# The opening of a Fourier-then-experts kernel on one core: units copied by two engines, a new order of its tail, and two transfer queues reordered

## The chip, the core and the metric

The kernel runs on one core of a Trainium2 chip. The core has a matrix engine (TensorE, PE in the profile, with its weight loads as PEld), a vector engine (VectorE, DVE), a scalar engine (ScalarE, ACT), a general engine (GpSimd, POOL) and a queue engine (SyncE, SP) that here only issues transfers. Each engine works through its own list of instructions in order. The engines share two memories on the core: SBUF, and PSUM, into which alone the matrix engine writes and which has eight banks of 128 x 512 floats. Sixteen DMA engines move data between these and DRAM. Transfers issued by SP stand in the profile as queue q1 (hardware_dynamic), those issued by POOL as queue q0 (software_dynamic).

The metric is the device time of one execution in microseconds. Before the change the median of three runs is 879.62 us (879.46 to 879.99).

## The reference

`x` has 8 batches of 3008 rows by 256. Each batch goes through a real FFT over the rows, a complex 256 x 256 product with bias, a soft threshold at 0.01, and the inverse FFT. The result, 24064 x 256, goes through two dense layers (256 to 2048 to 256) with an ELU between them.

```python
X = np.fft.rfft(x, axis=1)
Yr = Xr @ w_r - Xi @ w_i + b_r
Yi = Xr @ w_i + Xi @ w_r + b_i
Yr = np.sign(Yr) * np.maximum(np.abs(Yr) - lam, 0.0)
Yi = np.sign(Yi) * np.maximum(np.abs(Yi) - lam, 0.0)
y = np.fft.irfft(Yr + 1j * Yi, n=3008, axis=1)
h = y.reshape(-1, 256) @ w_in
out = np.where(h > 0, h, np.exp(np.minimum(h, 0)) - 1) @ w_out
```

## The kernel before

The FFT of 3008 = 47 x 64 rows is done as two matrix products with a turn of the data through DRAM between them, and the inverse likewise. That gives five kinds of unit for each batch `b`, written as functions.

- `unit_A(b, u)`, six of them: the first product on a part of `x` (tile `xt`), copied from PSUM (`aps`) to the tile `A` and written to DRAM (`DA`), two units to one write of 512 KB.
- `load_Z`: reads `DA` back, turned, into the tile `Z`.
- `unit_X(b, u)`, eight: the second product, copied from PSUM (`xps`) into `XT`.
- the complex product, bias and threshold, twelve groups. In the opening it is `first_M(q, i, on_act)` (L325), which ends in the tile `Y` of pair `q`. With `on_act` false, DVE adds the bias (L231), and POOL clips (L335) and subtracts (L336). With `on_act` true, the bias comes in by a fifth matmul (L218), ACT takes a relu into the tile `clip` (L332), and DVE combines both (L322). That last step is not issued at once: it is put into `held` and issued by `let_go`, which the next group calls. The tile `clip` has two buffers for both kinds.
- `unit_B(b, v)`, six (called `fB` in the opening): the first product of the inverse, copied from PSUM (`bps`) into `Bz` and written to DRAM (`DB`); `load_Bs(b, w)` reads it back turned, for one quarter `w` of the batch; `unit_Y(b, u)`, eight, does the second product into `yT`, the input of the dense layers.

For the first quarter of batch 0 (`w` = 0) only half of `Bs` comes through DRAM (`load_Bs(0, 0, K1 // 2)`, which needs the writes of B units 0, 1 and 2). The other half is computed by `quarter_B(v)`, v = 3 to 5, from a padded matrix (`M3p`, filled by `pad_M3`) and sent straight from SBUF to SBUF (L418).

The order in the opening is written out by hand (L767 to L848): each engine issues its part of each call in that order, so a call's place in the list is its place in the queues of PE, ACT, DVE, POOL and SP at once. A wait in the SP queue holds all transfers issued behind it. PSUM in the opening is three pools: `pre2` (two buffers of two banks, for the units), `pre1` (three buffers of one bank, tag `mps1`) and `pre0` (one bank, tile `ips`, for matmuls whose result is not used, `idle_pe`). `gate(src)` is a small POOL copy that holds POOL's next transfers until `src` is there. The weights come in quarters: `load_w_in(q)` and `load_w_out`, on POOL but for `load_w_in(0)` on SP; `scale_w_in` turns a quarter of `w_in` into bf16.

After the opening comes a main loop of 376 steps. Step `i` does two blocks of `h` (L903, PSUM `hps`), their ELU on ACT, POOL and DVE (L920, L925, L937), and the second layer for step `i` - 2 (L955). A planner (`units`, `plan`) puts one unit of the FFT work into each step. For the start its list is fixed: A units 4 and 5 of batch 1 in steps 1 and 2, the Y units 2 to 6 of batch 0 in steps 3 to 7, then the eight X units of batch 1 from step 8 on. Step 3 needs `load_Bs(0, 1)`, which needs the writes of all six B units; step 8 needs the first `load_Z(1, ...)`, which needs all three `DA` writes of batch 1.

Of the kernel before, what the change touches and what calls it, by code (L numbers as in the profile page):

```python
# [15 lines left out]
N1 = 47  # L16
# [9 lines left out]
def kernel(  # L26
# [168 lines left out]
    def unit_X(b, u, alone=False, on_dve=False):  # L195
        g, dt = u // 2, u % 2
        if u == 0:
            XT_of[b] = xtp.tile([P, 2, 2, K1 * N2], BF16, name="XT", tag="XT")
        XT, Z = XT_of[b], Z_of[b]
        ps = unit_ps("xps", alone)  # L200
        psv = ps[:].rearrange("p a (k j) -> p (a k) j", j=P)
        for kk in range(8):
            k = 8 * g + kk
            nc.tensor.matmul(  # L204
                psv[:, kk, 0 : 4 * K1], lhsT=Z[:, k, dt * P : dt * P + P],
                rhs=M2[:, k].rearrange("p c m -> p (c m)"), start=True, stop=True,
            )
        xv = XT[:, dt].rearrange("p c (m s) -> p c m s", s=NS)[:, :, :, 8 * g : 8 * g + 8]
        pv = psv[:, :, 0 : 4 * K1].rearrange("p k (c m) -> p c m k", c=2)
        later(alone, lambda: evac(xv, pv, on_dve))  # L210

    mps_of = {}

    def m_group(b, q, i, ps, biased=False):
        XT = XT_of[b]
        o = (2 * q + i) * P
        if biased:
            nc.tensor.matmul(ps, lhsT=busy[:, 0:P], rhs=bias_p, start=True, stop=False)  # L218
        for m, (c, wm) in enumerate(((0, wcat_r), (1, wcat_s))):
            for dt in range(2):  # L220
                nc.tensor.matmul(  # L221
                    ps, lhsT=XT[:, dt, c, o : o + P], rhs=wm[:, dt, :],
                    start=(not biased and m == 0 and dt == 0), stop=(m == 1 and dt == 1),
                )
        if i == 0:
            Y_of[b, q] = wk3.tile([P, 2, 2 * D], BF16, name="Y", tag="Y")
        if biased:
            yb = ps
        else:
            yb = wk3.tile([P, 2 * D], F32, name="yb", tag="yb")[:]  # L230
            nc.vector.tensor_tensor(yb, ps, bias_bc[:], ALU.add)  # L231
        clip = wk2.tile([P, 2 * D], F32, name="clip", tag="clip")
        return yb, clip

    Xd_of = {}

# [88 lines left out]
    def first_M(q, i, on_act):  # L325

        ps = pre1.tile([P, 2 * D], F32, name="mps1", tag="mps1")
        yb, clip = m_group(0, q, i, ps[:], on_act)
        let_go()
        Y_ = Y_of[0, q][:, i, :]  # L330
        if on_act:
            nc.scalar.activation(clip[:], yb, AF.Relu, bias=lam_n[:])  # L332
            held.append((Y_, yb, clip))
        else:
            nc.gpsimd.tensor_scalar(clip[:], yb, LAM, -LAM, ALU.min, ALU.max)  # L335
            nc.gpsimd.tensor_tensor(Y_, yb, clip[:], ALU.subtract)  # L336

    def unit_B(b, v, alone=False, on_dve=False):
# [6 lines left out]
        ps = unit_ps("bps", alone)  # L345
        psj = ps[:].rearrange("p s (q d) -> p (s q) d", d=D)
        if b < 2:
            Y = Y_of.pop((b, v))[:]
            if b == 1:
# [1 line left out]
            for pp in range(2):  # L351
                for c in range(2):
                    for s in range(2):
                        nc.tensor.matmul(
                            ps[:, s, pp * D : pp * D + D],
                            lhsT=M3f[c][s * N2 : s * N2 + N2, 2 * v + pp, :],
                            rhs=Y[s * N2 : s * N2 + N2, pp, c * D : c * D + D],
                            start=(c == 0), stop=(c == 1),
                        )
# [7 lines left out]
        def done():  # L367
            o = 4 * (v % 2)
            Bv = Bz[:, o : o + 4, :].rearrange("p (q s) d -> p s q d", s=2)
            psv = ps[:].rearrange("p s (q d) -> p s q d", d=D)  # L370
            if on_dve:
                nc.scalar.copy(Bv[:, :, 0], psv[:, :, 0])
                nc.vector.tensor_copy(Bv[:, :, 1], psv[:, :, 1])
            elif b < 2:
                nc.scalar.copy(Bv, psv)
            else:
                nc.scalar.copy(Bz[:, o : o + 4, :], psj)  # L377
            if alone or (b == 1 and v > 3):
                k0 = 4 * v
                nc.sync.dma_start(  # L380
                    DB_of[b][k0 : k0 + 4].rearrange("k p d -> p k d"), Bz[:, o : o + 4, :]
                )
            elif v % 2:
# [3 lines left out]
        later(alone, done)  # L387

    def load_Bs(b, w, k1=K1):

# [29 lines left out]
    def unit_Y(b, u, alone=False):  # L420
# [4 lines left out]
        ps = unit_ps("yps", alone)  # L425
        psv = ps[:].rearrange("p a (k j) -> p (a k) j", j=P)
        for j in range(8):
            nc.tensor.matmul(  # L428
                psv[:, j, 0 : 2 * N1], lhsT=Bs[:, j, dt * P : dt * P + P], rhs=M4[:],
                start=True, stop=True,  # L430
            )
        yv = yT[:, dt, w * WT : w * WT + WT].rearrange("p (r j) -> p r j", j=8)
        pv = psv[:, :, 0 : 2 * N1].rearrange("p j r -> p r j")
        cut = TB // 8 if alone else 2 * N1

        def done():
            nc.scalar.copy(yv[:, 0:cut], pv[:, 0:cut])  # L437
            if alone:
                nc.vector.tensor_copy(yv[:, cut:], pv[:, cut:])  # L439

        later(alone, done)

# [630 lines left out]
    def plan():  # L1073
# [129 lines left out]
```

## Time and profile before

| | us |
|---|---|
| median of three runs | 879.62 |
| the profiled execution, its own time | 878.99 |
| its span, first to last instruction | 877.0 |
| PE busy in the span | 860.4 (98%) |
| ACT, POOL, DVE busy | 725.0, 658.1, 656.4 |
| first matmul of the main loop (step 0) | 53.05 |
| first X unit of batch 1 (step 8) | 70.82 |

All times in the rows are from the start of the span. A row of the timeline gives the start, the duration, the engine, the line, the operation, the tiles (out<-in) and in brackets how long the engine had been idle and what ended that. A row of the chain of waits gives start, duration and the work that was the last to be waited for. A row of the DMA view gives for one stretch a queue's packets, MB and the time that they took as a share of 16 engines. SPq rows are SP's issues: their duration is that of the issue, not of the transfer.

### The profile page before, as it was taken

The page shows a single profiled execution, that of the slowest core. Times are in us where ns is not written, and L with a number is a line of the kernel's source. Part 1 is how long each engine was busy: PE and PEld are TensorE (multiplying, and loading weights), DVE is VectorE, ACT ScalarE, POOL GpSimd, SP SyncE. Part 2 cuts the span into 40 slices and gives each one's busy share as a digit, 9 for nine tenths or more (in the row PEclk, how much of TensorE's full clock was granted, in tenths as well). Part 3 has the DMA queues.
Part 4 walks back from the last instruction along what each step waited for, and adds up shares of the span by engine and source line. Part 5 has one row for each costly group of instructions (what it writes and reads, how often), then busy time and mean ns, then how long its engine had stood idle before and what let it go on. Part 6 is the DMA issues. An engine that isn't in the chain of part 4 may idle for free.

```text
span 877.0 us, 20405 instructions
## 1 busy us (share of the span) xinstructions
PE 860.4 (98%) x7677; PEld 701.8 (80%) x7794; DVE 656.4 (75%) x1072; ACT 725.0 (83%) x1218; POOL 658.1 (75%) x994
## 2 busy tenths in 40 slices
PE   8989999999999999999999999999999999999997
PEld 3457777878888888988889888898888988888886
DVE  8686886678767787677876778767776788777775
ACT  6678998889888997899978998789987888786664
POOL 7736995679667987698866888678885699756664
PEclk9999999999999999999999999999999999999999
DMA  8995336733485245642564344553444123421101
GB/s 273 344 257 147 113 105 190 224 102 101 121 234 175 74 134 161 183 134 77 151 176 136 118 132 116 151 169 97 137 118 133 31 62 85 133 75 30 48 27 49
DMA packets 106579, 116.68 MB, mean 133 GB/s; under 512 B 11041, under 2 KB 96545, under 8 KB 103601
## 3 DMA queue, kind: packets, MB, share of 16 engines
q1 hardware_dynamic: 99856, 86.28, 35.6%
q0 software_dynamic: 6480, 28.97, 10.6%
q8 instruction: 61, 1.00, 0.5%
q14 instruction: 38, 0.30, 0.1%
q10 hardware_dynamic: 144, 0.13, 0.0%
HBM read 55.12 MB, written 49.81 MB: 120 GB/s over the span
## 4 chain that ended last, share of the span: by engine, by line
PE 85%; POOL 5%; DVE 4%; DMA 3%; issue 1%; ACT 1%; POOLq 0%; SPq 0%; DVEq 0%; ACTq 0%
PE ps_o L955 37%; PE hps L903 32%; PE mps L269 5%; PE aps L168 3%; PE xps L204 3%; PE yps L428 2%; POOL Et L925 2%; PE bps L363 1%; DMA Z<-DA 1%; POOL Y L300 1%; DVE gT L937 1%; DMA DA<-A 1%; PE mps L221 1%; DVE yb L286 1%; POOL yb L295 1%
## 5 line engine op out<-in xcount | busy, mean ns | idle before, releaser
L937 DVE SCALAR_TENSOR_TENSOR gT<-Et,hps 128x512 fp32r<-128x512 f32 x752 | 493.8, 684 | 162.9 <-POOL Et L925 161.8
L955 PE MATMUL ps_o<-w_out_r,gT 128*128 128x256 f32 x3008 | 472.5, 299 | 0.1
L925 POOL TENSOR_SCALAR Et<-Et 128x512 f32<-128x512 f32 x578 | 351.8, 616 | 147.2 <-ACT Et L920 145.6
L955 PEld LDWEIGHTS ps_o<-w_out_r,gT 128*128 128x128 f32 x3008 | 399.0, 188 | 46.3 <-DVE gT L937 0.3
L920 ACT ACTIVATE Et<-hps 128x512 f32<-128x512 f32 x584 | 343.9, 605 | 96.4 <-PE hps L903 92.9
L903 PE MATMUL hps<-yT,w_in_s 128*128 128x512 bf16 (+9 forms) x2671 | 417.1, 279 | 1.5 <-DVE yT L439 0.8
L903 PEld LDWEIGHTS <-w_in_s 128*128 128x128 bf16 x2783 | 163.1, 98 | 57.1 <-issue 13.4
L917 ACT ACTIVATE Et<-hps 128x512 f32<-128x512 f32 x168 | 99.7, 593 | 19.0 <-PE hps L903 18.3
L918 ACT ACTIVATE Et<-Et 128x512 f32<-128x512 f32 x168 | 106.1, 632 | 5.3
L300 POOL TENSOR_TENSOR Y<-yb,clip 128x512 bf16<-128x512 f32 x84 | 108.5, 1292 | 0.3
L295 POOL TENSOR_TENSOR yb<-yb,bias_d 128x256 f32<-128x256 f32 x68 | 49.8, 732 | 28.4 <-DVE yb L286 28.0
L296 POOL TENSOR_SCALAR clip<-yb 128x512 f32<-128x512 f32 x84 | 51.6, 614 | 13.2 <-DVE yb L282 6.7
L253 POOL TENSOR_TENSOR Xd<-XT 128x256 bf16<-128x256 bf16 x84 | 56.5, 672 | 0.0
L437 ACT CAST yT<-yps 128x752 bf16<-128x752 f32 (+1 forms) x64 | 49.5, 774 | 3.0 <-PE yps L428 3.0
L269 PE MATMUL mps<-wsum,XT 128*128 128x256 bf16 x336 | 50.4, 273 | 0.0
L131 ACT CAST A<-aps 128x1024 bf16<-128x1024 f32 (+1 forms) x46 | 45.6, 992 | 5.4 <-PE aps L168 5.3
L131 ACT CAST XT<-xps 128x768 bf16<-128x768 f32 x60 | 47.7, 795 | 2.7 <-PE xps L204 2.5
L286 DVE TENSOR_TENSOR yb<-mps,Kb 128x512 f32<-128x512 f32 x68 | 47.0, 692 | 2.6
L285 DVE TENSOR_TENSOR Kb<-mps,bias_bc 128x256 f32<-128x256 f32 x68 | 28.7, 422 | 25.0 <-PE mps L269 25.0
L168 PE MATMUL aps<-xt,M 128*128 128x512 f32 x96 | 38.0, 481 | 1.2 <-DMA xt<-in_x_dram 0.4
L428 PEld LDWEIGHTS <-Bs 96*128 96x128 bf16 x512 | 27.8, 98 | 13.7 <-issue 1.8
L377 ACT CAST Bz<-bps 128x1024 bf16<-128x1024 f32 x36 | 36.3, 1008 | 0.0
(128 smaller groups left out, 504.7 us busy)
## 6 DMA issues: line engine op xcount, KB each, us to landing
xt<-in_x_dram POOLq DMA_DIRECT2D x21, 1024.0 KB, 5.5
out_dram<-osb SPq DMA_DIRECT2D x158, 128.0 KB
Bs<-DB SPq DMA_DIRECT2D x31, 384.0 KB
DA<-A SPq DMA_DIRECT2D x21, 512.0 KB
Z<-DA SPq DMA_DIRECT2D x27, 384.0 KB
DB<-Bz SPq DMA_DIRECT2D x20, 512.0 KB
Yt<-Y SPq DMA_DIRECT2D x144, 64.0 KB
xt<-in_x_dram POOLq DMA_DIRECT2D x6, 512.0 KB, 6.0
```

The lines of the kernel that those rows point to most:

```text
L131: nc.scalar.copy(dst, src)
L168: nc.tensor.matmul(two[j], lhsT=M1[:], rhs=xt[:, 4 * uu + 2 * j : 4 * uu + 2 * j + 2, :], start=True, stop=True,)
L269: nc.tensor.matmul(dst, lhsT=lhs(dt), rhs=rhs(dt), start=dt == 0, stop=dt == 1)
L295: nc.gpsimd.tensor_tensor(yb[:, D : 2 * D], yb[:, D : 2 * D], bias_d[:], ALU.add)
L300: nc.gpsimd.tensor_tensor(Y_, two(yb), two(clips[0]), ALU.subtract)
L903: nc.tensor.matmul(hps[s][:, a:z], lhsT=w_in_s[:, dt, ft * P : ft * P + P], rhs=yT_of[b][:, dt, t0 + a - c0 : t0 + z - c0], start=(dt == 0 ...
L917: nc.scalar.activation(e, h, AF.Relu, scale=-1.0)
L918: nc.scalar.activation(e, e, AF.Exp, scale=-1.0)
L920: nc.scalar.activation(e, h, AF.Exp)
L925: nc.gpsimd.tensor_scalar(e, e, 1.0, 0.0, ALU.min, ALU.max)
L937: nc.vector.scalar_tensor_tensor(g_of[self.i][:, p], self.E[:, p], -1.0, self.h[p], ALU.add, ALU.max)
L955: nc.tensor.matmul(po[q][:, i_ % 2, :], lhsT=gT[:, s, i_ * P : i_ * P + P], rhs=w_out_r[:, ft, :], start=(ft == 0 and i_ % 2 == 0), stop=( ...
```

## The change

1. X unit 7 gets two PSUM tiles of `pre1` instead of one of `pre2`; ACT copies one half, DVE the other. Before, DVE copied it whole.
2. The relu of the groups (q, 1), q < 5, goes into a tile of its own, `Kb` (one buffer), and no longer shares the two `clip` buffers with POOL.
3. The B unit that two engines copy (`fB(5, True)`) gets two `pre1` tiles, one for each engine.
4. Y unit 0 gets two PSUM tiles (`ips` and one of `pre1`), copied by ACT and DVE; Y unit 1 is copied by ACT alone. Before, each was copied by ACT and then DVE from one tile.
5. The tail is reordered: `pad_M3` in two parts, earlier; the two halves of `scale_w_in(2)` move from the main loop (DVE) into the opening (ACT); `first_M(5, 1)` goes ahead of `quarter_B(3)`; `quarter_B(4)` and `quarter_B(5)` go ahead of `fB(4)`; one `idle_pe` goes.
6. On SP, `load_Bs(0, 0)` goes ahead of the DB write of B unit 3, which waits in `late_B` until after `quarter_B(5)`; `load_Bs(0, 1)` and `load_Bs(0, 2)` go ahead of the first `DA` write of batch 1. A unit 3 goes behind the Y units; the engines that copy the A units change.
7. On POOL, `load_w_in(1)` and `load_w_in(2)` go ahead of the three loads of `x`.

```diff
-        ps = unit_ps("xps", alone)
-        psv = ps[:].rearrange("p a (k j) -> p (a k) j", j=P)
+        if alone and u == 7:
+            two = [pre1.tile([P, 512], F32, name="xps", tag="mps1")[:] for _ in range(2)]
+            two = [t.rearrange("p (k j) -> p k j", j=P) for t in two]
+        else:
+            ps = unit_ps("xps", alone)
...
+            for a in range(2):
+                pv = two[a][:, :, 0 : 4 * K1].rearrange("p k (c m) -> p c m k", c=2)
+                evac(xv[:, :, :, 4 * a : 4 * a + 4], pv, bool(a))
...
+        if own:
+            return yb, wk1.tile([P, 2 * D], F32, name="Kb", tag="Kb")
...
+        if on_dve:
+            two = [pre1.tile([P, 512], F32, name="bps", tag="mps1")[:] for _ in range(2)]
...
+                if alone and v == 3:
+                    late_B.append(write)
+                else:
+                    write()
...
+        apart = alone and u == 0
+        if apart:
+            two = [ips[:], pre1.tile([P, 512], F32, name="yps", tag="mps1")[:]]
...
     gate(Z_of[0][:, 0, 0:1])
+    load_w_in(1)
+    load_w_in(2)
     for ci in range(3):
         load_x(1, ci)
-    load_w_in(1)
     load_w_out(0, 1)
-    load_w_in(2)
     load_w_out(1, 2)
...
     first_M(1, 1, True)
+    for h in range(2):
+        pad_M3(0, h)
     first_M(2, 0, False)
     fB(0)
     first_M(2, 1, True)
+    scale_w_in(0, True)
+    scale_w_in(2, False, slice(0, FQ // 2))
     first_M(3, 0, False)
     fB(1)
     first_M(3, 1, True)
-    for c in range(2):
-        for h in range(2):
-            pad_M3(c, h)
+    scale_w_in(2, False, slice(FQ // 2, FQ))
+    for h in range(2):
+        pad_M3(1, h)
     first_M(4, 0, False)
     fB(2)
     first_M(4, 1, True)
-    scale_w_in(0, True)
+    scale_w_in(1, True)
     first_M(5, 0, True)
-    quarter_B(3, True)
+    first_M(5, 1, True)
+    let_go()
+    quarter_B(3, False)
+    load_Bs(0, 0, K1 // 2)
     fB(3)
-    first_M(5, 1, True)
-    scale_w_in(1, True)
-    let_go()
-    quarter_B(4, False)
+    quarter_B(4, True)
+    quarter_B(5, True)
+    late_B.pop()()
     fB(4)
-    load_Bs(0, 0, K1 // 2)
-    idle_pe(1)
-    quarter_B(5, True)
     fB(5, True)
...
-    gate(Bz_of[0, 2][:, 6, 0:1])
+    gate(Bz_of[0, 2][:, 5, 0:1])
     load_w_in(3)
     load_w_out(2, 3)
-    unit_A(1, 0, ahead=True, both="sd")
-    unit_A(1, 1, ahead=True)
+    unit_A(1, 0, ahead=True)
     for w in (1, 2):
         load_Bs(0, w)
-    unit_A(1, 2, ahead=True, on_dve=True)
-    unit_A(1, 3, ahead=True, both="dd")
+    unit_A(1, 1, ahead=True, on_dve=True)
+    unit_A(1, 2, ahead=True, both="sd")
     for u in range(2):
         unit_Y(0, u, alone=True)
+    unit_A(1, 3, ahead=True, on_dve=True)
     gate(Bs_of[0, 1][:, 0, 0:1])
     load_w_out(3, 4)
...
-            f1[2 + c].append((scale_w_in, (2, True, slice(FQ // 2 * c, FQ // 2 * c + FQ // 2))))
```

More of the change, by code (lines that the diff above doesn't have):

```diff
@@ L212, with m_group @@
     mps_of = {}
-    def m_group(b, q, i, ps, biased=False):
+    def m_group(b, q, i, ps, biased=False, own=False):
         XT = XT_of[b]
@@ L327, in first_M @@
         ps = pre1.tile([P, 2 * D], F32, name="mps1", tag="mps1")
-        yb, clip = m_group(0, q, i, ps[:], on_act)
+        yb, clip = m_group(0, q, i, ps[:], on_act, on_act and i == 1 and q < 5)
         let_go()
@@ L344, in unit_B @@
         Bz = Bz_of[b, v // 2]
-        ps = unit_ps("bps", alone)
-        psj = ps[:].rearrange("p s (q d) -> p (s q) d", d=D)
+        if on_dve:
+            two = [pre1.tile([P, 512], F32, name="bps", tag="mps1")[:] for _ in range(2)]
+        else:
+            ps = unit_ps("bps", alone)
+            psj = ps[:].rearrange("p s (q d) -> p (s q) d", d=D)
+            two = [ps[:, s] for s in range(2)]
         if b < 2:
@@ L387, in unit_B @@
         later(alone, done)
+    late_B = []
     def load_Bs(b, w, k1=K1):
@@ L424, in unit_Y @@
         yT, Bs = yT_of[b], Bs_of[b, w]
-        ps = unit_ps("yps", alone)
-        psv = ps[:].rearrange("p a (k j) -> p (a k) j", j=P)
+        apart = alone and u == 0
+        if apart:
+            two = [ips[:], pre1.tile([P, 512], F32, name="yps", tag="mps1")[:]]
+        else:
+            ps = unit_ps("yps", alone)
+            two = [ps[:, a] for a in range(2)]
+        two = [t.rearrange("p (k j) -> p k j", j=P) for t in two]
         for j in range(8):
             nc.tensor.matmul(
-                psv[:, j, 0 : 2 * N1], lhsT=Bs[:, j, dt * P : dt * P + P], rhs=M4[:],
+                two[j // 4][:, j % 4, 0 : 2 * N1], lhsT=Bs[:, j, dt * P : dt * P + P], rhs=M4[:],
                 start=True, stop=True,
@@ L432, in unit_Y @@
         yv = yT[:, dt, w * WT : w * WT + WT].rearrange("p (r j) -> p r j", j=8)
-        pv = psv[:, :, 0 : 2 * N1].rearrange("p j r -> p r j")
-        cut = TB // 8 if alone else 2 * N1
         def done():
-            nc.scalar.copy(yv[:, 0:cut], pv[:, 0:cut])
-            if alone:
-                nc.vector.tensor_copy(yv[:, cut:], pv[:, cut:])
+            if apart:
+                for a in range(2):
+                    pv = two[a][:, :, 0 : 2 * N1].rearrange("p j r -> p r j")
+                    evac(yv[:, :, 4 * a : 4 * a + 4], pv, bool(a))
+                return
+            pv = ps[:].rearrange("p a (k j) -> p (a k) j", j=P)[:, :, 0 : 2 * N1]
+            nc.scalar.copy(yv, pv.rearrange("p j r -> p r j"))
         later(alone, done)
```

21 lines of the change are left out of this document (12 added, 9 removed).

## The prediction

> **What bounds the kernel now.** The page's first part and the windows come first: they tell where PE is the bound.
>
> ```profile
> PE 860.4 (98%) x7677; PEld 701.8 (80%) x7794; DVE 656.4 (75%) x1072; ACT 725.0 (83%) x1218; POOL 658.1 (75%) x994
> ```
>
> ```profile
> 36.00:38.00 2.00, 2.00 (x16) 0.85 (x15) 0.69 (x1) 0.08 (x1) 1.92 (x3) 1.00 1.19 402
> ...
> 50.00:52.00 2.00, 0.79 (x15) 0.59 (x15) 2.00 (x3) 0.03 (x1) 0.73 (x1) 1.00 0.86 163
> ...
> 66.00:68.00 2.00, 2.00 (x21) 1.64 (x20) 1.28 (x2) 1.66 (x3) 2.00 (x3) 1.00 1.16 240
> ```
>
> Columns after the stretch: its length, then the busy time of PE, PEld, DVE, ACT and POOL, the clock, the DMA share, GB/s. PE is full in the threshold groups (36 to 38) and from step 3 on, but not at 50 to 52, and the clock is 1.00 in all three. Nothing after step 8 is edited, and PE is the bound there; so the change is worth what it moves the start of step 8. The PE timeline and the chain of waits tell what sets that.
>
> ```profile
> 53.05 1.47 PE L903 MATMUL hps<-yT,w_in_s 128*128 128x512 bf16 x13 [0.78 <-DVE yT L439]
> ...
> 59.73 0.51 PE L428 MATMUL yps<-M,Bs 96*128 96x94 bf16 x8 [0.93 <-DMA Bs<-DB]
> ...
> 70.82 0.51 PE L204 MATMUL xps<-M,Z 96*128 96x96 bf16 x8 [0.26 <-DMA Z<-DA]
> ```
>
> ```profile
> 28.51 0.97 DVE XT L129
> ...
> 34.24 0.54 PE bps L354 x8
> ...
> 51.44 0.51 PE yps L428 x8
> ...
> 58.23 5.55 DMA DA<-A
> ...
> 63.97 6.80 DMA Z<-DA
> ```
>
> Three gates follow one another: the first Y unit at 51.44 (step 0 at 53.05), the second quarter's `Bs` at 59.73, and `Z` at 70.82. At the last PE waits only 0.26 us, but that wait is the end of a chain of two transfers (`DA` out at 58.23, `Z` in from 63.97) that fills 12.5 us: whatever brings steps 0 to 7 forward is lost unless those transfers come forward too. So I read SP's queue and, per microsecond, the two DMA queues.
>
> ```profile
> 35.86 5.54 SPq L380 DMA_DIRECT2D DB<-Bz  x3
> ...
> 45.36 0.36 SPq L380 DMA_DIRECT2D DB<-Bz  x1
> 46.21 0.61 SPq L418 DMA_DIRECT2D Bs<-Xd  x1
> 47.12 0.36 SPq L380 DMA_DIRECT2D DB<-A  x1
> 47.65 0.38 SPq L394 DMA_DIRECT2D Bs<-DB  x1
> 48.08 0.55 SPq L418 DMA_DIRECT2D Bs<-Xd  x1
> 49.00 0.36 SPq L380 DMA_DIRECT2D DB<-A  x1
> 49.82 0.36 SPq L184 DMA_DIRECT2D DA<-A  x1
> 52.41 1.01 SPq L394 DMA_DIRECT2D Bs<-DB  x2
> 53.52 5.08 SPq L184 DMA_DIRECT2D DA<-A  x2
> ```
>
> ```profile
> 49.17 0.80 POOL L737 DMA_DIRECT2D w_in_f<-in_moe_w_in_dram  x1
> ```
>
> The next fence holds q1 in 36:44 and 44:45, then q0 and q1 in 52:53, q1 in 54:55 and in 61:62.
>
> ```profile
> q1 hardware_dynamic: 1321, 0.66, 32.6%
> ...
> q1 hardware_dynamic: 235, 0.11, 40.1%
> ...
> q0 software_dynamic: 55, 0.23, 75.7%
> ...
> q1 hardware_dynamic: 12, 0.01, 2.0%
> ...
> q1 hardware_dynamic: 465, 0.24, 82.0%
> ...
> q1 hardware_dynamic: 664, 0.34, 118.0%
> ```
>
> Two things are to be seen. The three writes of B units 0 to 2 (issued from 35.86) are 3 x 512 packets of 512 bytes, and 1321 + 235 packets bring their end to shortly before 45: the weights and `x` on q0 hold them up. And when POOL's `w_in(3)`, issued at 49.17, moves (52:53), q1 nearly stops, with a `DA` write pending since 49.82; it recovers at 54.
>
> **The change, part by part.**
>
> *X unit 7 on two tiles.* The groups wait for its DVE copy (28.51, 0.97 us). Halved, ACT's part starts after its own copy of unit 6:
>
> ```profile
> 27.74 0.80 ACT L131 CAST XT<-xps 128x768 bf16<-128x768 f32 x1
> ...
> 41.32 0.38 PE L218 MATMUL mps<-spare 128*128 128x512 bf16 x1 [0.17 <-DVE yb L231]
> ...
> 45.86 0.38 PE L410 MATMUL bps<-Y,M3p 128*128 128x256 bf16 x2 [0.16 <-DVE w_in_s L753]
> 46.70 0.38 PE L410 MATMUL bps<-Y,M3p 128*128 128x256 bf16 x2 [0.46 <-DVE Y L322]
> 47.55 1.19 PE L168 MATMUL aps<-xt,M 128*128 128x512 f32 x4
> ```
>
> at 28.5, and takes about 0.45 (half of 0.80 and a fixed part): 28.95 instead of 29.48. Gain 0.5; below, 0.3 if the strided half costs as much as two thirds.
>
> *Groups and B units.* From there to the end of the last B unit (47.55) PE is a queue with stalls of 0.17, 0.16 and 0.46 and one `idle_pe` (0.23), about 1.0 in all. The tile `Kb` takes ACT's relu off POOL's clip buffers, where it waited up to 2.08:
>
> ```profile
> 37.92 0.69 ACT L332 ACTIVATE clip<-mps,lam_n 128x512 f32<-128x512 f32 x1 [2.08 <-POOL Y L336]
> ...
> 39.24 1.30 DVE L398 COPY M3p<-M3f 64x192 bf16<-64x192 bf16 x4
> ...
> 42.12 1.59 POOL L336 TENSOR_TENSOR Y<-yb,clip 128x512 bf16<-128x512 f32 x1
> ...
> 48.28 0.69 DVE L373 CAST A<-bps 128x512 bf16<-128x512 f32 x1 [0.74 <-ACT A L372]
> ```
>
> With it and the earlier pads (1.30 of DVE in two parts) the stalls go; POOL's five pairs run without their gap, the last at about 40.9 instead of 42.12. One new wait of 0.2 appears: B unit 0 on POOL's first `Y`, which the head start doesn't move. So the last B unit ends at 47.55 - 0.5 - 1.0 + 0.2 = 46.2. `quarter_B(5)` stands two B units earlier in the list (2 x 0.54): out of PE at 45.1, copied at 45.7. The two halves of `scale_w_in(2)` on ACT, 0.6 each, lie in its idle stretch (0.08 busy of 36:38); without that cover they'd cost 1.2. What they leave in steps 2 and 3, two DVE copies, was behind the 0.93 wait of step 3 and gains nothing. The B unit on two tiles takes out the 0.74 that DVE waited for ACT; its write comes at about 47.3 instead of 49.0 if nothing else holds SP.
>
> *Weights ahead of `x`.*
>
> ```profile
> DMA to landing us min/median/max: 8.3/10.9/13.1
> ```
>
> That is the three loads of `x`, issued from 23.10. `w_in(1)` and `(2)` in their place land like the first, at some 31 to 33; ACT wants the second at 36.4. `x` comes 1 MB later, the last at 40 instead of 37.4 and wanted from 46.2 on. The bytes ahead of the three DB writes stay the same, so these still land near 46. Cost nothing; if `w_in(2)` came after 37, ACT and the B copies behind it would slip by the excess.
>
> *SP's queue.* `load_Bs(0, 0)` must wait for the third DB write: end of data before 45, and 1.2 until it is seen (the write of 49.00 is seen at 52.41, its packets end at 51). So SP stands at it until 46.1, though `Xd` and `Bz` tiles are ready from 45. Then, at the spacings of the rows: load 46.1, `quarter_B(4)` 46.5, `quarter_B(5)` 47.1, the late write 47.7, then the last two DB writes 48.0 and 48.4. The last `Xd` transfer took 3.3 from issue to the first Y unit (48.08 to 51.44), with a DB write ahead of it that is now behind: 2.5 to 3.3. The first Y unit starts at 49.6 to 50.4, I take 49.7: 1.7 earlier. Y unit 0's two copies run side by side and unit 1's follows whole (0.8); yT is ready 1.7 after the start, as before (1.6). Step 0 starts near 51.4.
>
> *What is late next.* POOL's gate is released by the last B copy, two us earlier, and `w_in(3)` goes out at 47.1 instead of 49.17: ahead of the three DB writes on SP, not behind them as before. In 52:53 such a load brought q1 to 12 packets. Of 1,536 packets some 300 pass before 49; then two us of nothing; then, with 465 in 54:55 as the best, some 310 in a us: the last is out near 55, seen at 56.2. `load_Bs(0, 1)`, at 52.41 before, is issued then, and the `DA` writes of A units 0 to 3, at 49.82 and 53.52 before, stand behind it. Two `Bs` loads of 0.39 MB at 0.25 MB per us end at 60; the first releases step 3 near 59.2 (59.73 before): of 1.7 us, 0.5 are left. The three `DA` writes, 1.57 MB at 0.34, end at 64.5 and are seen at 65.3, against 63.8 before. That is the worse end, 1.5 later. The other end counts bytes: all that must move from 45 on is the same, q0's part starts 2.0 earlier and 0.6 MB of DB writes come 2 us later at 0.3: nothing lost. The nearest row to either is 52:53, in which q1 really stood; but the later us run faster with q0 done. I take the middle: `Z` and step 8 come 0.7 later.
>
> **The sum.** The head starts (0.5 on the groups, 1.7 at the Y unit) end in waits at steps 3 and 8: +0.7 us against the profiled execution's 878.99 (span 877.0 and 2.0 around it), so 879.7; the median of the runs is 0.63 above that execution, which makes 880.3.
>
> **The rivals.**
>
> *The transfers come forward as well* (faster). If the DB writes, issued at most 1.3 us after `w_in(3)`, are still let through, they are seen at 52.5, `Bs` lands near 56.5, the 0.93 wait of step 3 goes, and the `DA` writes end by 61.5: step 8 comes 2.1 earlier, 877.5. For it: `w_in(3)`'s own packets came 1.9 after its issue. Against it: the `DA` write issued 0.65 after `w_in(3)` stood. 0.25.
>
> *The queues share* (a little faster). Each queue keeps about half of the 0.3 MB per us: the DB writes end at 53.3 instead of 55, and step 8 comes 0.7 earlier, 878.9. [...] 0.15.
>
> *The last weights meet the `DA` writes* (slower). `load_w_out(3, 4)` goes out when `Bs(0, 1)` lands. Before, that was at 59.97, behind the last `DA` write (58.23), and `Z` then took 6.8 us:
>
> ```profile
> 59.97 0.75 POOL L742 DMA_DIRECT2D w_out_r<-in_moe_w_out_dram  x1
> ```
>
> If `Bs(0, 1)` lands before the third `DA` write is issued (about 58), the 512 KB go ahead of the `DA` writes and hold them as `w_in(3)` held one: 2 us and more, 1.6 of them on top of my 0.7: step 8 2.3 later, 881.9. Against it: I have `Bs` land at 59.2. 0.17.
>
> *It doesn't do what it says.* If the third DB write lands after 47.5, `load_Bs(0, 0)` gains nothing from its new place, the two `Xd` transfers stand behind it, and the Y unit starts at 51 or later; the rest shifts with it: 881.0. Against it: the packets end before 45. 0.08.
>
> **How the numbers follow.** The likeliest is 880.3, its own range 879.4 to 881.1 (step 8 from 0.2 earlier to 1.5 later); it has 0.35. Within 0.2% of the median (877.9 to 881.4, about what a measurement of this kernel can tell from no change) lie it, the sharing case and the case without effect, less their tails, together 0.57. Faster: the first rival and a tail of the second, 0.26. Slower: the third and a tail of the likeliest, 0.17. The range reaches half into the first rival and to the third, 877.2 to 881.8, and leaves out some 0.2.
>
> **What would show it.** Right: the first group near 29.0, `quarter_B(5)`'s copy near 45.7, the first Y unit at 49.6 to 50.4, step 0 near 51.4; q1 near nothing at 49 to 51; `load_Bs(0, 1)` issued at 55 or later; a PE wait of over 2 us for `Bs` in step 3, and one for `Z` of over 0.5 before step 8. Wrong: `load_Bs(0, 1)` issued before 53.5, or the first X unit of batch 1 before 69.5. A relu or B copy on ACT that waits for `w_in_f` would break the part on the weights, and a first group later than 29.3 that on X unit 7.

## The result, and the profile after

The changed kernel takes 882.52 us (median; 881.17 to 884.73), the kernel before in the same series 879.71: a ratio of 1.003, 95% interval 1.0022 to 1.0037. It is slower by 0.3%; the forecast was 880.3, a small loss within what can be measured. The profiled execution took 881.32, with a span of 879.0 (before: 878.99 and 877.0).

First the engines' busy times on the page of the changed kernel, then its PE timeline (start, busy time, count, and in brackets the idle time in front of it and what ended it):

```profile
PE 861.1 (98%) x7677; PEld 702.8 (80%) x7793; DVE 655.5 (75%) x1068; ACT 727.1 (83%) x1221; POOL 658.8 (75%) x994
```

```profile
49.10 0.33 PE L453 MATMUL ips<-M,Bs 96*128 96x94 bf16 x4 [1.72 <-DMA Bs<-Xd]
...
50.80 1.47 PE L933 MATMUL hps<-yT,w_in_s 128*128 128x512 bf16 x12 [0.34 <-ACT yT L466]
...
56.99 0.73 PE L168 MATMUL aps<-xt,M 128*128 128x512 f32 x2 [3.06 <-ACT A L131]
...
59.91 0.51 PE L453 MATMUL yps<-M,Bs 96*128 96x94 bf16 x8 [0.34 <-DMA Bs<-DB]
...
69.67 0.51 PE L453 MATMUL yps<-M,Bs 96*128 96x94 bf16 x8 [1.30 <-DMA Bs<-DB]
...
72.39 0.51 PE L209 MATMUL xps<-M,Z 96*128 96x96 bf16 x8 [0.39 <-DMA Z<-DA]
```

The sums of busy time hardly move; the waits do. Y unit 0 starts at 49.10 instead of 51.44 and step 0 at 50.80 instead of 53.05. Then PE waits 3.06 for a copy of ACT, 0.34 and 1.30 for `Bs`, 0.39 for `Z`, and step 8, the last place that the edit can reach, begins at 72.39 instead of 70.82. The chain of waits names the transfers:

```profile
23.12 0.96 DVE XT L129
...
28.44 0.59 PE mps L231 x2
...
48.16 7.66 DMA DB<-A
...
55.90 3.96 DMA Bs<-DB
...
59.91 0.51 PE yps L453 x8
...
68.56 3.79 DMA Z<-DA
...
72.39 0.51 PE xps L209 x8
```

The third of the last DB writes takes 7.66 us from issue to being seen. And on POOL's queue, SP's queue and ACT of the same kernel:

```profile
46.47 0.80 POOL L764 DMA_DIRECT2D w_in_f<-in_moe_w_in_dram  x1
...
60.15 0.75 POOL L769 DMA_DIRECT2D w_out_r<-in_moe_w_out_dram  x1
```

```profile
45.62 1.25 SPq L438 DMA_DIRECT2D Bs<-Xd  x2
46.97 0.54 SPq L394 DMA_DIRECT2D DB<-Bz  x1
47.56 1.13 SPq L394 DMA_DIRECT2D DB<-A  x2
55.90 0.79 SPq L414 DMA_DIRECT2D Bs<-DB  x2
56.80 4.73 SPq L184 DMA_DIRECT2D DA<-A  x3
...
68.56 1.26 SPq L193 DMA_DIRECT2D Z<-DA  x3
```

```profile
55.93 1.01 ACT L131 CAST A<-aps 128x1024 bf16<-128x1024 f32 x1 [2.91 <-DMA DB<-A]
```

`w_in(3)` goes out at 46.47, ahead of all three DB writes (46.97 to 48.16), and SP stands until 55.90 for them. ACT's copy of A unit 4 needs a tile that the last two of these writes still read, so it waits as well (2.91), and with it PE.

One thing has to be taken off before the two executions are compared. The copy of X unit 1 on DVE started at 23.12 here and at 23.68 before. Of what is edited only POOL's reordered loads are issued ahead of it, from 22.4, and their first packets move after 25 in both executions:

```profile
23.68 0.96 DVE XT L129
```

Over all profiles of this study, of either kernel, it started between 23.07 and 24.14. The opening up to there varies by itself, and this execution had 0.56 us of luck against that of the kernel before. From there to step 8 it is 49.27 us after and 47.14 before: the change costs 2.13 in this execution, not 1.57. From step 8 to the end of the span it is 805.8 to 807.2 us in all sixteen profiles (806.6 after, 806.2 before), with both orders spread over that range: behind step 8 the profiles show nothing of the change beyond their scatter.

### The profile page after: what moved, and what is told of

Read it like the earlier page. It is cut to its first block, busy times and chain, and to the rows that moved or that the text cites. A ratio compares the mean times of both kernels' runs of the same rounds, so it can differ in the third digit from the quotient of the medians.

```text
span 879.0 us, 20396 instructions
## 1 busy us (share of the span) xinstructions
PE 861.1 (98%) x7677; PEld 702.8 (80%) x7793; DVE 655.5 (75%) x1068; ACT 727.1 (83%) x1221; POOL 658.8 (75%) x994
## 4 chain that ended last, share of the span: by engine, by line
PE 83%; POOL 8%; DVE 3%; DMA 3%; issue 2%; ACT 1%; POOLq 0%; DVEq 0%; SPq 0%
PE ps_o L985 36%; PE hps L933 31%; PE mps L280 5%; PE xps L209 3%; PE aps L168 2%; POOL Et L955 2%; PE yps L453 2%; POOL Y L311 2%; PE bps L378 1%; POOL clip L307 1%; DVE gT L967 1%; PE mps L231 1%; DMA Z<-DA 1%; POOL yb L306 1%; POOL Xd L264 1%
## 5 line engine op out<-in xcount | busy, mean ns | idle before, releaser
L933 PE MATMUL hps<-yT,w_in_s 128*128 128x512 bf16 (+8 forms) x2671 | 417.2, 279 | 0.9 <-ACT yT L466 0.3
L306 POOL TENSOR_TENSOR yb<-yb,bias_d 128x256 f32<-128x256 f32 x68 | 49.7, 731 | 28.3 <-DVE yb L297 27.6
L264 POOL TENSOR_TENSOR Xd<-XT 128x256 bf16<-128x256 bf16 x84 | 56.5, 673 | 0.0
L131 ACT CAST A<-aps 128x1024 bf16<-128x1024 f32 (+1 forms) x46 | 45.6, 993 | 7.7 <-PE aps L168 4.6
L466 ACT CAST yT<-yps 128x752 bf16<-128x752 f32 x63 | 49.2, 781 | 1.3 <-PE yps L453 1.2
L131 ACT CAST XT<-xps 128x768 bf16<-128x768 f32 (+1 forms) x61 | 48.1, 790 | 2.3 <-PE xps L209 2.3
L1000 DVE COPY osb<-ps_o 128x512 f32<-128x512 f32 x46 | 31.7, 690 | 6.2 <-PE ps_o L985 5.1
```

The costliest lines, as they stand in the source:

```text
L131: nc.scalar.copy(dst, src)
L264: nc.gpsimd.tensor_tensor(Xd_of[b, k][:], XT[:, :, 0, o : o + P], XT[:, :, 1, o : o + P], ALU.subtract)
L933: nc.tensor.matmul(hps[s][:, a:z], lhsT=w_in_s[:, dt, ft * P : ft * P + P], rhs=yT_of[b][:, dt, t0 + a - c0 : t0 + z - c0], start=(dt == 0 ...
```

## The experiments

"Difference" below is the median of a kernel less that of the kernel before in the same series; "to step 8" is the distance from X unit 1's copy to the X unit of step 8 in the profiled execution, less the 47.14 of the kernel before. The kernels are called e1 to e14 in the edits (e2 has another tile, e3 another tile and the gate moved). A profile shows one execution. Those of e4 and e5 are the fastest of their ten, that of e9 is the slowest and that of e12 the slowest but one; so the profiles tell which waits there are, and the medians what an edit is worth.

### The gate of the early weights, on both kernels

```diff
 changed kernel, e1
-    gate(Bz_of[0, 2][:, 5, 0:1])
+    gate(Bs_of[0, 0][64:96, 0, 0:1])
 kernel before, e4
-    gate(Bz_of[0, 2][:, 6, 0:1])
+    gate(Bz_of[0, 2][:, 0, 0:1])
```

> The changed kernel with POOL's gate ahead of w_in(3) moved from the last B copy to the landing of the last Xd transfer (48.85 us in the changed kernel's trace), so that w_in(3) is issued at about 49.0 instead of 46.47, behind all six DB writes. Theory (w_in(3), issued ahead of the last three DB writes, holds them): the DB writes are seen by about 52 instead of 55.8, load_Bs(0, 1) is issued at about 52, A unit 4's copy no longer waits, the first X unit of batch 1 starts at 70.0 to 70.8 (72.39 in the changed kernel) and the time falls to about 880.5. Rival (it is SP's new order, with the DA writes behind the Bs reads, that costs): step 8 stays at 72 or later and the time at 882.5.

> The kernel before, with the gate ahead of w_in(3) moved from the copy of B unit 5 to that of B unit 4, so that w_in(3) is issued near 47.2 instead of 49.17, ahead of the last DB write (49.0); nothing else changes. Theory of w_in(3): that DB write is seen at 54 or later instead of 52.4, load_Bs(0, 1) goes out then, step 3 starts at 60.5 or later (59.73), step 8 0.5 to 1.5 later than 70.82, time 880.2 to 881.2. Rival (the order on SP costs, the gate doesn't): step 8 within 0.3 of 70.82, time 879.7.

The changed kernel with `w_in(3)` behind the last `Xd` transfer (and `w_out(2, 3)`, which stands behind the same gate) took 880.2: 1.0012 (1.0001 to 1.0022), a difference of 1.0 instead of 2.8, to step 8 +0.11. `w_in(3)` went out at 50.13, the DB writes were seen at 51.98 instead of 55.90, and the wait of 3.06 fell to 0.31. The rival, that SP's new order costs, is left with at most the 1.0 that remains (0.1 to 1.9 by the interval). The kernel before with the gate alone moved forward took 881.77: 1.0025 (1.0016 to 1.0034), a difference of 2.6, to step 8 +2.56, more than the 0.5 to 1.5 expected. POOL, SP and PE of it:

```profile
46.86 0.80 POOL L737 DMA_DIRECT2D w_in_f<-in_moe_w_in_dram  x1
```

```profile
48.56 0.36 SPq L380 DMA_DIRECT2D DB<-A  x1
49.38 0.36 SPq L184 DMA_DIRECT2D DA<-A  x1
55.86 0.79 SPq L394 DMA_DIRECT2D Bs<-DB  x2
```

```profile
54.12 1.05 PE L428 MATMUL yps<-M,Bs 96*128 96x94 bf16 x16 [4.34 <-issue]
...
62.30 0.50 PE L428 MATMUL yps<-M,Bs 96*128 96x94 bf16 x8
```

SP stands until 55.86, as in the changed kernel, but here that is not what costs. The load also went out in front of the last `Xd` transfer, which was issued at 47.64 and landed only at 53.92 (before: 48.08 and 51.24). So the first Y unit came at 54.12 instead of 51.44, and from there PE reached step 8 without another wait for a transfer. The Y unit alone is 3.1 us later, counted from X unit 1's copy, than in the kernel before. So one move explains most of the loss: the head start brings POOL's gate forward, and the two loads then run in front of small transfers that are wanted sooner. That the early loads cost was shown from both sides; that they cost by way of the DB writes was seen in the changed kernel alone, and on the old order they cost by way of `Xd`.

### The tile of A units 4 and 5

```diff
-                t = "Bz" if b == 2 and ci == 2 else "A"
+                t = "Bz" if b in (1, 2) and ci == 2 else "A"
```

> The changed kernel with the tile of A units 4 and 5 of batch 1 taken from the other buffer pair (Bz), whose DB writes are long done, so that ACT's copy of unit 4 doesn't wait for the last DB writes (3.06 us of PE in the changed kernel). If that wait is on the path (it puts the third DA write behind w_out(3, 4)): the third DA write goes out near 57.8, ahead of w_out(3, 4) at 60.1, step 8 starts near 71.0 and the time falls by about 1.4 to 881.1. If the wait is covered by the later wait for Bs(0, 1) at 59.9: step 8 within 0.3 of 72.39, time 882.5.

> Both edits. Theory of w_in(3): with the gate moved the DB writes are seen at 52, before unit 4's copy wants its tile, so the tile adds nothing: same as e1 within 0.3 us. If the tile's wait is a cause of its own: up to 1.4 us faster than e1.

With another tile for these units 0.30 of the 3.06 is left, in an execution whose Y units came so late that A unit 5 might not have waited with the old tile either. The time is 882.02 (1.0026, 1.0016 to 1.0037): a difference of 2.8, as without the edit. With the gate moved as well it is 879.98 (1.001, 0.9999 to 1.002), not to be told from the gate alone. The wait was one more place where the late DB writes showed, not a cause. The profile of the tile alone held something else:

```profile
53.01 0.47 PE L453 MATMUL ips<-M,Bs 96*128 96x94 bf16 x4 [5.57 <-DMA Bs<-Xd]
```

```profile
52.00:54.00 2.00, 0.99 (x14) 1.02 (x15) 0.17 (x1) 0.47 (x1) 0.00 (x0) 0.50 1.28 320
54.00:56.00 2.00, 2.00 (x15) 1.21 (x13) 0.93 (x2) 0.79 (x1) 0.00 (x0) 0.50 0.78 233
```

(The second fence is of the stretches: length, busy time of PE, PEld, DVE, ACT and POOL, clock, DMA share, GB/s.) In this execution `w_in(3)` went out just ahead of the last `Xd` transfer (46.52 against 47.05), so that the first Y unit came at 53.01. In the changed kernel's profile it went out 0.15 behind it (46.47 against 46.32). Nothing orders the two, and an execution can fall either way. And the clock fell to 0.50 in the long idle time of PE, at 50.7, and stayed there until 57.5. That points at the changed kernel's other executions: 14 of 16 have a mean clock of 0.996 or less (median 0.9945; its profiled one 0.999, the kernel before 0.998 in the median). The three with the lowest clocks (0.992, 0.993 and 0.993) are the three slowest (883.18 to 884.73). The profiled execution is one of the lucky ones. By an estimate, 3.4 us at half clock (50.2 to 53.6 in the kernel with the gate moved) lower the mean of an execution of 880 us by 0.002, so that 0.9945 is what 6.8 us or more of it make, as in this profile (mean 0.995). That suggests, without showing it, that many of the changed kernel's executions had the late Y unit as well.

### Keeping PE busy ahead of the first Y unit

```diff
+    idle_pe(16)        # e5, on the changed kernel; 11 with the gate moved (e6)
     for u in range(2):
         unit_Y(0, u, alone=True)
```

> The changed kernel with 16 idle matmuls (0.216 us each, 3.45 in all) on PE ahead of the first Y unit, so that PE isn't idle while it waits for the last Xd transfer; nothing else is changed. Theory of the clock: a PE gap of some 2.4 us or more there makes the granted clock fall to 0.5 for 3 us and more (0.50 from 50.5 to 53.5 in the run with the gate on Xd, whose gap was 2.42; not in the profiled execution of the changed kernel, whose gap was 1.72), and in most of the changed kernel's other executions it did so too: their mean clock is 0.992 to 0.997 against 0.999 in the profiled one. By it the clock of this kernel's executions is 0.996 to 0.998 and the time 881.3 (2.0 over the kernel before, the part that the transfers cost). Rival: PE waits for Bs in step 3 in any case, so the slower clock costs nothing: 882.5, whatever the clock is.

> The changed kernel with the gate on the last Xd transfer (as before, 880.2) and 11 idle matmuls (2.4 us) ahead of the first Y unit. Theory of the clock: the clock stays at 1.00 from 50 to 54, step 0 starts near 51.4 instead of 52.92. Since Bs(0, 1) lands at 59.4 as before, most of that ends in a longer wait of PE in step 3, 2.5 us instead of 1.18; the X unit of step 8 at 70.0 to 70.3; 879.3 to 880.0. Rival, that the clock cost this kernel its head start: the time falls by 1.5, to 878.7.

The clock behaved as expected: 0.997 to 0.999 in all executions of both. The time followed little: 881.9 (1.0022, 1.0012 to 1.0032) and 880.15 (1.0006, 0.9997 to 1.0016), 0.5 less each than without the filling, when taken against the kernel before, and inside the intervals. In the profile of the first the filling itself held the Y unit up: the last `Xd` transfer had landed at 49.55, and the 16 idle matmuls ran until 51.69. So that run gives the price of the clock less the price of the delay. In the second, step 0 started at 52.03, which is 28.2 us behind X unit 1's copy, as expected (51.4 was meant with the copy at 23.07: 28.3), and not 29.9 as with the gate alone. PE then waited 0.83, 0.58 and 0.75 for `Bs` twice and for `Z`: the later waits took the gain. The stretches of the kernel with the gate alone, where PE had waited 2.42, show what the filling prevents:

```profile
50.00:52.00 2.00, 2.00 (x17) 1.27 (x15) 0.71 (x2) 1.26 (x2) 1.56 (x2) 0.55 0.86 230
52.00:54.00 2.00, 1.78 (x13) 1.17 (x13) 1.59 (x3) 1.01 (x2) 0.00 (x0) 0.60 0.91 197
54.00:56.00 2.00, 1.69 (x9) 0.79 (x8) 1.95 (x4) 2.00 (x4) 0.00 (x0) 1.00 1.23 318
```

PE is all but full from 50 to 54 and, at a clock of 0.50 from 50.2 to 53.6, does about half the work: two matmuls of A, 128x512 f32, took 1.20 at 50.60 and 0.63 at 46.71, where the clock was 1.00. That is why its step 0 came at 52.92 and not near 51.

### The weights where the DMA engines are free

```diff
 changed kernel, e7 and e8 (with idle_pe(12) ahead of the Y units)
-    gate(Bz_of[0, 2][:, 5, 0:1])
+    gate(Bz_of[0, 1][:, 0, 0:1])
     load_w_in(3)
+    gate(Bs_of[0, 0][64:96, 0, 0:1])      # e8 only
     load_w_out(2, 3)
```

> The changed kernel with the gate of w_in(3) and w_out(2, 3) on the copy of B unit 2, so that both go out at 42.9 and 43.7, when the DMA engines are busy a fifth of the time and the third DB write is already under way, and 12 idle matmuls ahead of the first Y unit. Theory of the order of transfers: the last three DB writes, with nothing in front of them, land at 50.5 to 51.5, load_Bs(0, 1) goes out then and lands at 55 to 56 instead of 59.9, so the waits in step 3 and in A unit 5 go; the Xd transfers stand behind the weights and the first Y unit slips to 50 to 51; the DA writes end by 62, Z is in by 67, the X unit of step 8 starts at 68.5 to 69.5 without a wait: 877 to 878.2. Rival, that the bytes decide and not their order: the same bytes must move before Z, so the X unit stays at 70.3 to 71 and the time at 879 to 880.

> As the kernel with both weights early, but only w_in(3) goes out at 42.9; w_out(2, 3) has a gate of its own on the last Xd transfer. Theory of the order: Xd is held by one load instead of two, the first Y unit starts at 49.5 to 50; w_out(2, 3) then goes out near 50, ahead of load_Bs(0, 1), which lands 1.7 later than with both early, at 57 to 58, still before step 3 wants it at 58.5; 877 to 878.5. If it is slower than the kernel with both early by over 0.5, the load on the way of Bs counts for more than the start of the Y unit. Rival, bytes alone: 879 to 880, as for the other.

With both loads early 879.46 (0.9995, 0.9985 to 1.0004), with `w_in(3)` alone early 878.67 (0.9986, 0.9976 to 0.9995). The first came out by the rival's numbers (X unit 0 at 70.74): the waits in A unit 5 and step 3 did go, but the `Xd` transfers stood behind two loads, and the third DA write (issued 58.27) behind `w_out(3, 4)` (57.31). The second is 0.2 over the theory's range, under the rival's, and faster than the kernel before by 0.9. POOL and SP of it:

```profile
43.02 0.80 POOL L764 DMA_DIRECT2D w_in_f<-in_moe_w_in_dram  x1
...
58.88 0.74 POOL L769 DMA_DIRECT2D w_out_r<-in_moe_w_out_dram  x1
```

```profile
51.89 0.80 SPq L414 DMA_DIRECT2D Bs<-DB  x2
52.79 6.16 SPq L184 DMA_DIRECT2D DA<-A  x3
```

With the load at 43.02 SP is let go at 51.89, four us before the changed kernel, and the last weights, at 58.88, follow the third DA write, which landed at 64.19 instead of 68.5. `Bs(0, 1)` still stood behind `w_out(2, 3)` (58.30), and PE waited 0.92 for it and 0.82 for `Bs(0, 3)`.

### The old order with the same gates

```diff
 kernel before, e10
-    gate(Bz_of[0, 2][:, 6, 0:1])
+    gate(Bz_of[0, 1][:, 0, 0:1])
     load_w_in(3)
+    gate(Bs_of[0, 0][64:96, 0, 0:1])
     load_w_out(2, 3)
```

> The kernel before with the gates of the split kernel: w_in(3) behind the copy of B unit 2 (POOL is free for it at 44.6), w_out(2, 3) behind the landing of the last Xd transfer. It tells what the changed kernel's head start is worth once the transfers are out of its way. If the gain of the split kernel (0.9 under the kernel before) is that of the loads' place alone: 878.7 here too. If it is the change's head start, released: the old order gets nothing from earlier loads, whose w_in(3) stands in front of its Xd transfers: Y unit at 51.4 or later, 879.3 to 880.

879.7 (1.0003, 0.9994 to 1.0013). With these gates the old order gains nothing, which speaks for the second reading: the gain of the split kernel is the change's head start, let through. It does not settle it, since this kernel has no filling. Its clock fell to 0.50 from 52.6 to 56.0 behind an idle time of 2.02, and from step 0 to step 8 PE then waited for no transfer that could have hidden this. The old order with the gates and the filling was not run.

### The last weights, and the DA write back in front

```diff
 e9, on the split kernel; e12 has the second part alone, e11 both
-    gate(Bs_of[0, 0][64:96, 0, 0:1])
-    load_w_out(2, 3)
 ...
     gate(Bs_of[0, 1][:, 0, 0:1])
+    load_w_out(2, 3)
     load_w_out(3, 4)
 second part: one piece of the change undone
     unit_A(1, 0, ahead=True)
+    unit_A(1, 1, ahead=True, on_dve=True)
     for w in (1, 2):
         load_Bs(0, w)
-    unit_A(1, 1, ahead=True, on_dve=True)
```

> The split kernel (w_in(3) at 42.9, 878.67) with w_out(2, 3) moved from the landing of the last Xd transfer to that of Bs(0, 1), just ahead of w_out(3, 4). Theory of the order of transfers: with no load in front of it Bs(0, 1), issued at 51.9, lands at 55 instead of 58.3, the wait of 0.92 in step 3 goes; the two weights, issued at 55.3 and 56.1, now go ahead of the third DA write (56.73) and hold it for some 3 us, so that it lands at 64 to 65 and Z's first part at 68 to 69, just when X unit 0 wants it: X unit at 69.2, 877.8 to 878.4. Rival, that the bytes decide: what Bs gains the DA write and Bs(0, 3) lose, the wait moves to step 7 or 8, and the time stays at 878.7 or rises to 879.5.

> The split kernel with the first DA write back ahead of the reads of Bs(0, 1) and (0, 2), as in the kernel before (one part of the change undone). SP stands idle for the seen DB writes from 49.0 to 51.9; the write goes out at 49 ahead of w_out(2, 3) (50.24) and lands near 52; load_Bs(0, 1) is issued at 51.9 as before. Theory: 0.5 MB less behind Bs, so Bs(0, 3) lands at 66 instead of 67.86 and the wait of 0.82 in step 7 goes; Bs(0, 1) lands 58 to 58.5 and step 3 keeps its wait: 877.8 to 878.4. Rival: the write stands in front of w_out(2, 3) and so of Bs(0, 1), which lands 1.7 later, at 60: 879.5 to 880.5; then the change's reads ahead of the writes are worth 1 us.

> Both edits: w_out(2, 3) behind Bs(0, 1) and the first DA write ahead of the two Bs reads, on the split kernel. By the theory of order the gains add: the first DA write goes at 49 while the DMA engines are half idle, so 0.5 MB less stands between 52 and 64, the third DA write lands at 62 to 63, Z at 66 to 67, no wait at steps 3, 7 and 8: 877 to 877.8. By the rival (bytes) 878.3 to 879.

Apart they gave 879.28 (0.9996, 0.9987 to 1.0005) and 878.82 (0.9996, 0.9987 to 1.0005), together 878.43 (0.999, 0.9981 to 1.0). In the first the wait of step 3 went, as expected, but the third DA write landed at 66.94, with both weights moving beside it, and `Bs(0, 3)` behind it, and waits of 1.23 and 0.83 came up in steps 7 and 8: the rival's number. In the second the write went ahead of `w_out(2, 3)`, `Bs(0, 1)` landed at 59.97, and step 3 waited 1.77: the rival's mechanism, in an execution of 879.98, while the median lies between the two. Together the first DA write went out in the free stretch at 49, the third landed at 62.07, and X unit 0 came 1.23 earlier (from X unit 1's copy) than in the kernel before. The median is in the rival's range all the same: `Z` landed at 69.43 and not at 66 to 67, with the weights ahead of it. In the medians that is no gain over the split kernel: both are 0.94 under the kernel before. So the order decides where PE waits, and as far as these three runs tell, no place for `w_out(2, 3)` gained beyond the split kernel: the same bytes stand in front of `Z`.

### The price of the clock, with no later wait to hide it

```diff
 on the kernel with both edits, which has idle_pe(12)
-    idle_pe(12)        # e13
-    idle_pe(12)        # e14
+    idle_pe(8)
```

> The kernel with both edits (878.43) without the 12 idle matmuls ahead of the first Y unit: PE is idle from 47.7 until the last Xd transfer lands at 50.3, 2.6 us. Theory of the clock: in most executions the granted clock falls to 0.5 for some 3.4 us behind that gap (mean clock of an execution 0.994 to 0.997 instead of 0.998 to 0.999), in which PE does half the work; as hardly a later wait is left to hide it (0.25 at step 8), the time rises by 1.0 to 1.7 against the kernel with 8 idle matmuls. Rival: the wait in step 8 and the copies hide it, as in the changed kernel with and without the gate on Xd: the same within 0.4.

> The same with 8 idle matmuls (1.7 us): a gap of 0.9 is left, no dip of the clock (mean 0.998 to 0.999), the first Y unit where Xd lets it start, at 50.0 to 50.3, X unit 0 of batch 1 at 69.0 to 69.5: 878.2 to 878.6, faster than the kernel before by 0.1%. If instead the filling itself delays the Y unit, this one is faster than the kernel with 12.

Without filling 878.64 (0.9989, 0.998 to 0.9998), with 8 idle matmuls 877.84 (0.9981, 0.9971 to 0.9991), on one chip against the same 18 executions of the kernel before. The mean clock was 0.995 to 0.998 without and 0.998 to 1.0 with. PE and two stretches, first without, then with:

```profile
50.92 0.33 PE L453 MATMUL ips<-M,Bs 96*128 96x94 bf16 x4 [2.52 <-DMA Bs<-Xd]
```

```profile
52.00:54.00 2.00, 1.44 (x13) 0.80 (x13) 1.23 (x1) 1.16 (x2) 0.00 (x0) 0.74 0.77 226
54.00:56.00 2.00, 2.00 (x7) 1.04 (x6) 1.85 (x4) 1.21 (x3) 0.00 (x0) 0.50 0.82 223
```

```profile
50.27 0.33 PE L453 MATMUL ips<-M,Bs 96*128 96x94 bf16 x4 [0.48 <-DMA Bs<-Xd]
...
68.79 0.51 PE L209 MATMUL xps<-M,Z 96*128 96x96 bf16 x8
```

```profile
52.00:54.00 2.00, 2.00 (x18) 1.21 (x18) 1.54 (x3) 1.39 (x3) 0.00 (x0) 1.00 0.83 226
54.00:56.00 2.00, 1.80 (x10) 0.73 (x8) 1.93 (x5) 2.00 (x5) 0.00 (x0) 1.00 0.92 275
```

The dip costs 0.8 in the medians, a little less than the 1.0 to 1.7 expected and twice what the rival allowed; the two intervals overlap, so its size is known only roughly. It also rests on this one pair. The kernel with 12 idle matmuls kept its clock too (0.998 to 0.999) and was only 0.94 under the kernel before, on another chip. Longer filling explains little of that: its Y unit came 0.41 after the last `Xd` landed, that with 8 idle matmuls 0.25. That the kernel with 8 came out under its expected 878.2 to 878.6 stays open as well. In the profile the loss came by a detour: A unit 5 was late, and its DA write went out behind the two weights (58.92 against 56.91) instead of between them. The run without filling also bears on the old order with early gates, which had no filling and a dip too: 1.1 under the kernel before here, 0.3 over there. The two differ in the place of `w_out(2, 3)` besides, but the old order is the slower one with the clock alike. The kernel with 8 idle matmuls beats both: 0.2% under the kernel before and, by the two ratios, some 0.5% under the changed one.

## Why the prediction was wrong, point by point

*The head starts were right.* With the 0.56 of luck put back, the part of the first group that waits for the halved copy starts at 29.0 (28.44 in the chain; forecast 29.0), `quarter_B(5)` is copied by 45.6 (45.7), the last B unit ends near 46.0 (46.2), the Y unit starts at 49.7 (49.7) and step 0 at 51.4 (51.4).

*Weights ahead of `x` and the halves on ACT* cost nothing that the traces show: no relu or B copy on ACT waits for `w_in_f`. That part was not tried alone.

*SP's queue was right to a third of a us*, with the luck put back: `load_Bs(0, 0)` at 45.8 (46.1), the three writes at 47.5, 48.1 and 48.7 (47.7, 48.0, 48.4), `w_in(3)` at 47.0 (47.1), `load_Bs(0, 1)` at 56.5 (56.2).

*The step that failed is "I take the middle".* Of the two ends for `Z`, 1.5 and 0, the text took 0.7; this execution has 2.13 with the luck off. The worse end was the right one, and it was still short by 0.6. Two things lie beyond it. The first is the term for the three `DA` writes, "1.57 MB at 0.34". The rows of the changed kernel are q1 in 61:62, then q0 and q1 in 63:64 and in 64:65:

```profile
q1 hardware_dynamic: 690, 0.35, 114.6%
...
q0 software_dynamic: 122, 0.12, 82.3%
q1 hardware_dynamic: 115, 0.05, 20.2%
...
q0 software_dynamic: 188, 0.19, 79.8%
q1 hardware_dynamic: 113, 0.06, 30.0%
```

The 0.34 was reached, but only until the packets of `w_out(3, 4)` came, some two us after its issue at 60.15; then q1 moved 0.05 and 0.06 MB per us. The third DA write, issued at 58.86, was seen only at 68.5 (forecast: 65.3), and `Bs(0, 3)`, for which PE waits 1.30 in step 7, landed behind it, at 69.6. `Z` made up for most of that: with the load already through, it took 3.8 instead of 6.8. That is the third rival, and its 2.3 is the nearest to what came. Its point of decision was wrong: I had let it act only if the load went out ahead of that write, and it acted although it went out 1.3 later. By these rows, what counted was how much was still to move when the load's own packets began. And the wait of 3.06 for a tile that the DB writes still read was not in the text at all; it took the place of the wait over 2 us that I had put at step 3, where only 0.34 was left, as only 0.39 of the "over 0.5" was for `Z`. The times with another tile show that the place does not matter.

*What a typical execution loses beyond the profiled one was not foreseen.* The median difference is 2.8, and the median lies 1.20 above the profiled execution, not 0.63 as the sum had it. The text itself has the last `Xd` load behind a copy at 47.1 and `w_in(3)` at 47.1, and drew nothing from it. Where the load comes first, the Y unit can come as late as in the 53.01 above. And the text priced the end of `idle_pe` and of the stalls at a gain, without asking what the longer idle time in front of the Y unit does to the clock; its price, by the one pair of runs above, is some 0.8 where little hides it. How the 0.7 between 2.13 and 2.8 divides between the two in the changed kernel was not separated.

*The rival in which the queues share* was wrong by its own arithmetic. It gave each queue half of the bytes. The two stretches 49 to 51 and 52 to 54 of the changed kernel have (packets, MB, share of 16 engines):

```profile
q0 software_dynamic: 101, 0.40, 88.8%
q1 hardware_dynamic: 112, 0.06, 9.5%
...
q0 software_dynamic: 452, 0.45, 83.6%
q1 hardware_dynamic: 436, 0.22, 47.3%
```

The packets are nearly even (101 to 112, 452 to 436), the bytes 7 to 1 and 2 to 1, since a packet of `w_in` has 4 KB (0.40 MB in 101), one of `w_out` 1 KB (0.45 MB in 452) and one of the DB writes 512 B (0.22 MB in 436). No run shows the half of the bytes; by an estimate, the shares of these rows in its place (0.06 of 0.46 MB, then 0.22 of 0.67) would have given the long hold of the DB writes that came, and so would have spoken for the worse end. Not every stretch is as even: in 52:53 of the kernel before q1 moved 12 packets and q0 55, in a us in which the `DA` write may not have begun, and in 54:55 q1 moved 465 and q0 67.

*The faster rival*, that the DB writes get through, is the opposite of what happened.

## What to carry to other kernels

A head start on the compute side also brings forward every transfer that is released by it: write down for each such load what it will now stand in front of, and gate it by the landing of the transfer that it must not pass. Put a load where the DMA engines are idle, not where its release happens to fall; the same edit was worth +2.8 us with the load in front of the last writes, and -1.9 with the loads moved, one `DA` write back in its old place and PE kept busy. And where a change lengthens an idle time of PE to some 2 us, look at the clock behind it (0.50 here behind 2.02 to 5.57), and in the clocks of all executions, since the one that is profiled may be the one without the dip.

## What the runs showed of the hardware

*The clock fell behind short idle times.* Behind idle times of PE of 2.02, 2.35, 2.42, 2.52, 4.34 and 5.57 us the granted clock fell to 0.50, in five of these six profiles for about 3.4 us (50.2 to 53.6 in the kernel with the gate moved) and behind the longest for 6.8 (50.7 to 57.5), at times only a us or two after PE had started again (at about 53.0, PE at 50.92, in the kernel without filling), and in the longest while it was still idle; behind 1.21 in the kernel before, and behind 1.72 and 3.06 in the changed kernel's profile, it stayed at 1.00. So the length alone does not decide. What else does, these runs do not show.

*Small writes waited for a large load on the other queue.* The last DB write took 3.3 us from issue to landing in the kernel before (49.00 to 52.27) and 7.7 in the changed one (48.16 to 55.83), with two loads of 0.5 MB in front of it (issued at 46.47 and 47.27); with those loads behind the last `Xd` transfer it was seen at 51.98 instead of 55.90. A write of 0.5 MB that was issued 1.3 us ahead of such a load and behind two others of its own queue was still held by it (the third DA write, 9.6 us, while q1 fell from 0.35 MB per us in 61:62 to 0.05 in 63:64). By what mechanism, no run here shows.

*The opening varies by 1.1 us* (23.07 to 24.14 for the same copy, over the profiles of both orders). A difference of one profiled execution has to be taken from a point behind it.
